# Expert 1 in one piece: block products for a whole expert behind the late half of expert 0, in a fused scan and mixture-of-experts kernel

## The chip, the cores and the metric

The kernel runs on one core of a Trainium2 chip. The metric is device time in microseconds, the median of several runs. Names of engines are those of the profile: PE multiplies matrices (PEld is its weight loading, which overlaps), DVE is the vector engine, ACT the scalar engine, POOL the general engine that also issues the gathers and scatters of rows, SP the queue that issues the plain transfers.

## The reference

Two blocks in a row. The first is a state-space scan over 4 batches, 8 heads and 768 positions, with 32 values and 16 states per head. Its output, 3072 rows of 256 values, is the input of a router: each row goes to the one of 8 experts whose embedding is nearest by cosine, and the row's result is the expert's two-layer network, scaled by the softmax weight of the chosen expert.

```python
xn = x / (np.linalg.norm(x, axis=-1, keepdims=True) + 1e-06)
logits = xn @ en.T / tau
expert_idx = np.argmax(logits, axis=1)
...
for e in range(E):
    mask = expert_idx == e
    h = np.maximum(x[mask] @ w1[e], 0.0)
    out[mask] = gate_w[mask, None] * (h @ w2[e])
```

Each expert has w1 of 256 x 1024 and w2 of 1024 x 256, all in float32. How many rows an expert gets depends on the data.

## The kernel before, in words

**The scan** (`mamba`, line 758) goes through the 768 positions in six chunks of 128. Each chunk ends with rows of 264 values: 256 outputs and 8 logits. `send_rows` writes the rows of a chunk (four batches x 128) to a table in device memory, `y_rows`.

**The routing** runs beside the scan, two or three chunks behind. `pick` finds the expert of each row, `count_picks` adds up the counts (POOL), `rank_rows` and `keep_ranks` give each row its rank within its expert (PE, then ACT), `places` turns ranks into one-hot tiles (DVE), and `locate` multiplies these (PE), which gives for each expert and each of its places the number of the row that belongs there. An expert has 4 tiles of 104 places. `end_places` (line 696) adds the parts of all chunks, transposes them with one product (`table`, line 692), and `to_rows` (line 708) makes two integer tables of that: `gi`, the rows to gather, and `to`, the rows of the output to write.

**Early and late halves.** The first two tiles of experts 0 and 1 can be filled from the first three chunks alone; `early_places` makes a table `gi0` for them while the scan still runs, and `gather_halves` gathers their rows on POOL. So the order of PE after the scan is

1. expert 0, early half: 8 up-projections `up(f)` (each two matmuls over 208 rows), mixed in `scan_end` (line 912) with the end of the routing; then `down(0)` and `down(1)`, 8 matmuls each;
2. expert 1, early half, the same way;
3. expert 0, late half, and expert 1, late half (`moe`, line 1377), for the two tiles each that could be filled only after the last table product;
4. experts 2 to 7, sorted by size, each whole (up to 416 rows).

**Block products.** Experts 2 to 7 use `up_blocks` and `down_blocks` (lines 1182, 1257): the matrices are split into 2 x 2 blocks and multiplied in seven block products in place of eight. A block product of the up-projection is four matmuls, so an expert has 28 + 28 matmuls of about 208 columns in place of 32 + 32. For that DVE makes four sums of blocks of w1 (`sum_w1`), of x (`sum_x`), of w2 (`sum_w2`) and of the hidden values (`sum_h`), and adds products up.

**Gates.** The class `Gates` (line 1326) makes the row weights from the gathered logits: squares (ACT), a power (POOL), differences and scales (DVE), `exp` (ACT), sums and reciprocals (DVE).

**Order.** These parts are written under a manual schedule: each engine runs its instructions in the order of the code, and waits in place. Weights come through SP in the order of the calls of `load_weights`; three buffers each hold w1 and w2. `hold` delays a transfer until a given instruction is done. POOL issues gathers (line 996) and the scatters of results (line 1317) in code order too.

Of the kernel before, what the change touches and what calls it, by code (L numbers as in the profile page):

```python
# [17 lines left out]
Q = 128  # L18
# [592 lines left out]
def keep_ranks(k, c):  # L611
    k.at[c] = k.work.tile([128, NB, E], F32, name="rk", tag="rk")
    k.nc.scalar.copy(out=k.at[c][:].rearrange("p b e -> p (b e)"), in_=k.pz[1][:, 392 : 392 + NB * E])
# [82 lines left out]
def end_places(k):  # L696
    nc = k.nc
    n = k.pz[1][:, 456 : 456 + E]
    nc.tensor.matmul(n, lhsT=k.ones[:], rhs=k.pre[:, NU, :], start=True, stop=True)
    nc.vector.tensor_copy(out=k.idx[:], in_=table(k))  # L700
    k.gi = k.const.tile([TR, E * NT], I32, name="gi")
    k.to = k.const.tile([TR, E * NT], I32, name="to")
    to_rows(k, k.idx[:, 0 : FIXED * NT], 0)
    k.n = k.const.tile([128, E], F32, name="n")
    nc.vector.tensor_copy(out=k.n[:], in_=n)


def to_rows(k, idx, at):
    nc = k.nc
    n = idx.shape[1]  # L710
    r = slice(at, at + n)
    nc.vector.tensor_scalar(out=k.gi[:, r], in0=idx, scalar1=-1.0, scalar2=0.0, op0=ALU.add, op1=ALU.max)
    none = k.mc.tile([TR, n], F32, name=f"none{at}")
    nc.vector.tensor_scalar(
        out=none[:], in0=idx, scalar1=0.0, scalar2=float(T + 1), op0=ALU.is_equal, op1=ALU.mult
    )
    out_rows(k, k.mc, k.gi[:, r], k.to[:, r], none[:], f"to{at}")


def sort_experts(k):  # L720
# [33 lines left out]
    nc.vector.reduce_sum(out=idx[:], in_=rows[:].rearrange("p s t e -> p (s t) e"), axis=AX.X)  # L754
    to_rows(k, idx[:], FIXED * NT)


def mamba(k):
# [41 lines left out]
    for c in range(NC):  # L800
# [50 lines left out]
        if c == NC - 1:  # L851
            k.early_x = early_rows(k)
            gather_halves(k, k.early_x, k.gi0, 0, 0, 3 * NB * Q)
        if c >= 2:
            count_picks(k, c - 2)
        if c == NC - 1:
            gather_halves(k, k.early_x, k.gi0, 0, 1, 3 * NB * Q)
            add_located(k, c - 3)
# [20 lines left out]
        if c == NC - 1:  # L879
            early = early_jobs(k)  # L880
            early[0].turn_x()
            rank_rows(k, c - 2)
            keep_ranks(k, c - 2)
# [3 lines left out]
        if c == NC - 1:  # L887
            load_weights(k, 0, (1,), early[0].turned)
            hold(k, send_rows(k, c - 1), early[0].turned)
            load_weights(k, 1, (0,), early[0].turned)  # L890
            early[0].w2, early[1].w1 = k.w2t[0], k.w1t[1]
# [20 lines left out]
def scan_end(k, early):  # L912

    nc = k.nc
    c = NC - 1
    first, second = early
    gates = Gates(k, k.ep, k.early_x, TR, NT)
    first.up(0)
    rank_rows(k, c - 1)
    keep_ranks(k, c - 1)  # L920
    first.up(1)
    finish(k, c)
    keep_rows(k, c)
    send_rows(k, c)
    load_weights(k, 1, (1,))
    second.w2 = k.w2t[1]
    places(k, c - 1)
    pick(k, c)
    count_picks(k, c)
    first.up(2)  # L930
    gates.square(0)
    first.up(3)
    gates.square(1)
    locate(k, c - 2, True, False)
    locate(k, c - 1, False, False)
    first.up(4)
    rank_rows(k, c)
    keep_ranks(k, c)
    places(k, c)
    for f in (5, 6):  # L940
        first.up(f)
        gates.square(f - 3)
    gates.power()
    gates.largest()
    gates.scale()
    first.up(7)
    second.turn_x()
    gates.exp()
    first.down(0)
    locate(k, c, False, True)  # L950
    end_places(k)
    late = late_jobs(k)
    first.down(1)
    g = gates.end()
    first.gate, second.gate = g[:, 0:HT], g[:, HT:]
    first.to, second.to = k.to[:, 0:HT], k.to[:, NT : NT + HT]
    for f in range(KF):
        second.up(f)
        if 1 <= f <= HT:
            first.out(f - 1)  # L960
        if f == HT:
            sort_experts(k)
            load_weights(k, FIXED)
    second.down(0)
    late[0].turn_x()
    second.down(1)
    k.step = k.ints("step", [128, LEFT], [[1, LEFT]], 0, 0)
    k.part = k.ints("part", [128, 1], [[0, 1]], 0, 1)
    return late
# [16 lines left out]
def early_rows(k):  # L986
    return k.ep.tile([TR, 2 * HT, KD * Y1], F32, name="xg", tag="xg", bufs=2)


def gather_halves(k, x, gi, t, e, rows=T):  # L990
    for i in range(HT):
        gather(k, x[:, HT * e + i, 0:W], gi[:, NT * e + t + i : NT * e + t + i + 1], rows)
# [41 lines left out]
def early_jobs(k):  # L1034
    k.pgs.close()
    ps = k.late_psum.enter_context(k.tc.tile_pool(name="early_ps", bufs=4, space=PSUM))
    k.next_bank = lambda: ps.tile([128, 512], F32, name="eb", tag="eb")
    jobs = []
    for e in range(2):
        j = Job(k, HT, TR, k.w1t.get(e), k.w2t.get(e), k.ep, k.next_bank)  # L1040
        j.x = k.early_x[:, HT * e : HT * e + HT, :]
        jobs.append(j)
    return jobs


def late_jobs(k):
    x = k.late_x = early_rows(k)
    for e in range(2):
        gather_halves(k, x, k.gi, HT, e)
    jobs = []  # L1050
    for e in range(2):
        j = Job(k, HT, TR, k.w1t[e], k.w2t[e], k.ep, k.next_bank)
        j.x = x[:, HT * e : HT * e + HT, :]
        j.to = k.to[:, NT * e + HT : NT * e + NT]
        jobs.append(j)
    return jobs


class Job:
# [41 lines left out]
    def up(s, f):  # L1101
# [8 lines left out]
        if f % 2 == 0 or s.bank_ is not None:  # L1110
# [4 lines left out]
    def down(s, j, half=None, fs=range(KF)):  # L1115
# [14 lines left out]
        if j % 2 == 0:  # L1130
# [246 lines left out]
def moe(k, second, late):  # L1377
# [6 lines left out]
    jobs = list(late)  # L1384
    for j in [second] + jobs:
        j.bank_ = None
    last, e, left = second, 1, leftover_blocks(k)
    for i in range(2):
        j = jobs[i]
        x = k.late_x if i == 0 else jobs[2].x  # L1390
        gates = Gates(k, k.ep if i == 0 else k.p, x, TR, NT)
        for f in range(KF):
            j.up(f)
            if 1 <= f <= last.nt:
                last.out(f - 1)
            if f == 3:
                e += 1
                jobs.append(begin(e))
            if 3 <= f < 7:
                gates.square(f - 3)  # L1400
        gates.power()
        gates.largest()
        last, n = j, jobs[i + 1]
        n.turn_x()
        gates.scale()
        gates.exp()
        j.down(0)
        g = gates.end()
        if i == 0:
            late[0].gate, late[1].gate = g[:, 0:HT], g[:, HT:]  # L1410
        else:
            n.gate = g
        j.down(1)
        if i == 1:
            n.sum_x()
            n.sum_w1(range(4))
        load_weights(k, i + 3)
    gates = None
    for i in range(2, E):
# [208 lines left out]
def kernel(  # L1628
# [24 lines left out]
    with ExitStack() as m:  # L1653
# [9 lines left out]
        with tc.manual_schedule():  # L1663
            early = mamba(k)
            late = scan_end(k, early)
    with (
# [4 lines left out]
        with tc.manual_schedule():  # L1671
            last = moe(k, early[1], late)
# [46 lines left out]
```

## Time and profile before

| what | value |
|---|---|
| time, median of 3 runs | 258.27 us (258.21 to 261.93) |
| the profiled execution | 262.64 us |
| its span, first to last instruction | 260.8 us |
| PE busy | 246.0 us (94%) |
| DVE, ACT, POOL busy | 66%, 46%, 47% |
| mean granted PE clock | 0.969 |
| traffic | 35.93 MB, mean 138 GB/s |

The page gives busy time per engine, the span in 40 slices, the DMA queues, the chain of work that ended last, and the costliest groups of instructions. Further views of the trace give the instructions in order of time and busy times by stage. A PE record for a float32 matmul appears twice, so that one matmul of 208 columns is two records. Times in the views count from the first instruction of the span.

### The profile page before, as it was taken

To read this page: it belongs to the slowest core of one execution; us is meant where nothing else is said; L and a number is where in the kernel's file an instruction comes from. 1 tells how busy PE (TensorE), PEld (TensorE's weight loads), DVE (VectorE), ACT (ScalarE), POOL (GpSimd) and SP (SyncE) were. 2 spreads that over 40 slices of the span, in tenths; PEclk is the share of its full clock that TensorE was granted. 3 is DMA by queue.
4 is the path that set the end of the run, shared out by engine and by line. 5 is a ranking of instruction groups with operands and counts; after the bars stand their busy time and mean duration, and the time that the engine had idled before them with its cause. 6 is when DMAs were issued, how large, how long until landed. Compare 5 with 4: busy or idle time off the path is not lost.

```text
span 260.8 us, 6970 instructions
## 1 busy us (share of the span) xinstructions
PE 246.0 (94%) x2692; PEld 222.6 (85%) x2692; DVE 171.7 (66%) x460; ACT 118.7 (46%) x344; POOL 121.8 (47%) x164
## 2 busy tenths in 40 slices
PE   7897999999699999999999999999999999999991
PEld 2676877878579899999979999999998998999890
DVE  6735689888455460334597896987988889784221
ACT  3524566774137041413255267248428427537400
POOL 5896373473702370648354138418525625125032
PEclk9979799999959999999999999999999999999998
DMA  4945476546299439498932393294176201001001
GB/s 141 326 146 196 147 249 190 182 134 157 70 263 269 139 86 241 153 218 237 220 122 70 77 260 88 49 260 130 52 187 189 74 5 40 24 0 40 23 20 39
DMA packets 22548, 35.93 MB, mean 138 GB/s; under 512 B 2777, under 2 KB 15780, under 8 KB 22512
## 3 DMA queue, kind: packets, MB, share of 16 engines
q1 hardware_dynamic: 19264, 28.73, 39.2%
q0 software_dynamic: 3088, 6.67, 9.6%
q8 instruction: 22, 0.36, 0.6%
q14 instruction: 14, 0.11, 0.1%
q10 hardware_dynamic: 160, 0.06, 0.1%
HBM read 29.05 MB, written 6.50 MB: 136 GB/s over the span
## 4 chain that ended last, share of the span: by engine, by line
PE 44%; issue 24%; POOL 16%; DVE 7%; DMA 5%; another core or an unknown queue 1%; POOLq 1%; ACT 1%; DVEq 0%; SPq 0%; ACTq 0%
POOL xg L996 8%; PE eb L1107 5%; POOL out_dram L1317 5%; PE pg L371 5%; DMA out_dram<-yo,to 4%; PE eb L1125 4%; PE yp L1194 4%; DVE g L381 4%; PE yp L1266 4%; PE hp L1107 3%; PE yp L1125 2%; PE hp L1194 2%; PE pz L438 2%; PE py L422 2%
## 5 line engine op out<-in xcount | busy, mean ns | idle before, releaser
L1317 POOL DMA_INDIRECT out_dram<-yo,to x32 | 34.0, 1061 | 66.1 <-ACT yo L1314 36.2
L996 POOL DMA_INDIRECT xg<-y_rows,gi x32 | 37.3, 1166 | 17.3 <-issue 9.1
L381 DVE TENSOR_TENSOR g<-pg,mask 128x1536 f32<-128x1536 f32 x12 | 21.1, 1757 | 10.0 <-PE pg L371 10.0
L1212 ACT ACTIVATE hT<-hT 128x416 f32<-128x416 f32 (+5 forms) x36 | 19.0, 532 | 12.6 <-DVE hT L1216 6.2
L1125 PE MATMUL yp<-hT,w 128*128 128x208 f32 (+1 forms) x128 | 22.1, 329 | 0.6 <-ACT hT L1212 0.6
L1125 PEld LDWEIGHTS yp<-hT,w 128*128 128x128 f32 x128 | 21.1, 190 | 0.8 <-ACT hT L1212 0.8
L1266 PE MATMUL yp<-T,S 128*128 128x208 f32 (+4 forms) x120 | 21.8, 332 | 0.0
L1266 PEld LDWEIGHTS yp<-T,S 128*128 128x128 f32 x120 | 20.4, 190 | 0.0
L1216 DVE TENSOR_TENSOR hT<-hp,u 128x416 f32<-128x416 f32 (+5 forms) x24 | 13.3, 564 | 10.6 <-PE hp L1194 4.3
L1344 POOL TENSOR_TENSOR gr<-gr,half 104x4 f32<-104x4 f32 x8 | 9.7, 1210 | 21.7 <-ACT sq L1338 21.6
L1194 PE MATMUL yp<-T,S 128*128 128x208 f32 (+5 forms) x96 | 18.6, 336 | 0.4 <-DVE S L1151 0.3
L283 POOL TENSOR_TENSOR xs<-x,rT 128x1024 f32<-128x1024 f32 x6 | 11.9, 1980 | 10.8 <-issue 7.6
L1194 PEld LDWEIGHTS yp<-T,S 128*128 128x128 f32 x96 | 15.4, 190 | 1.7 <-ACT u L1207 1.1
L1107 PE MATMUL eb<-xT,w 128*128 128x208 f32 x64 | 14.5, 375 | 2.2 <-ACT xT L1097 2.2
L1207 ACT COPY p<-yp 128x416 f32<-128x416 f32 (+5 forms) x12 | 5.7, 478 | 21.0 <-PE yp L1194 21.0
L1266 PE MATMUL yp<-hT,w 128*128 128x208 f32 (+4 forms) x80 | 15.1, 331 | 0.0
L1107 PEld LDWEIGHTS eb<-xT,w 128*128 128x128 f32 x64 | 12.0, 207 | 2.5 <-ACT xT L1097 2.3
L1266 PEld LDWEIGHTS yp<-hT,w 128*128 128x128 f32 x80 | 13.7, 190 | 0.0
L1338 ACT ACTIVATE sq<-xg 104x256 f32<-104x256 f32 x32 | 13.0, 408 | 0.0
L1107 PE MATMUL hp<-xT,w 128*128 128x208 f32 x64 | 12.2, 339 | 0.0
L433 ACT COPY yT<-py 128x512 f32<-128x512 f32 x12 | 6.5, 593 | 12.4 <-PE py L422 12.4
L1207 ACT COPY u<-yp 128x416 f32<-128x416 f32 (+5 forms) x24 | 11.5, 484 | 1.3 <-PE yp L1194 0.9
(285 smaller groups left out, 588.8 us busy)
## 6 DMA issues: line engine op xcount, KB each, us to landing
w<-in_moe_w_dram SPq DMA_DIRECT2D x32, 256.0 KB
w<-in_moe_w_dram SPq DMA_DIRECT2D x8, 1024.0 KB
y_rows<-rows SPq DMA_DIRECT2D x6, 528.0 KB
x<-in_x_dram SPq DMA_DIRECT2D x6, 512.0 KB
ct<-in_CT_dram SPq DMA_DIRECT2D x6, 256.0 KB
bi<-in_BT_dram SPq DMA_DIRECT2D x6, 256.0 KB
b<-in_B_dram SPq DMA_DIRECT2D x6, 256.0 KB
xa<-in_x_dram SPq DMA_DIRECT2D x6, 128.0 KB
```

The costliest lines, as they stand in the source:

```text
L371: t.paired = k.nc.tensor.matmul(k.pg[:, q, 192 * u + a : 192 * u + a + n], lhsT=m, rhs=x, start=True, stop=True, tile_position=(32 * q, 0),)
L381: t.masked = k.nc.vector.tensor_tensor(out=g[:], in0=k.pg[:, :, 0:384].rearrange("p q (u m) -> p q u m", u=2), in1=k.mask[:].unsqueeze(1). ...
L996: k.nc.gpsimd.indirect_dma_start(out=x, out_offset=None, in_=k.y_d[0:rows, :], in_offset=bass.IndirectOffsetOnAxis(ap=at, axis=0), bounds_ ...
L1107: nc.tensor.matmul(t, lhsT=s.w1[:, j, 128 * f : 128 * f + 128], rhs=s.xT[:, j, 0:m], start=(j == 0), stop=(j == KD - 1))
L1125: nc.tensor.matmul(t, lhsT=s.w2[:, f, 128 * j : 128 * j + 128], rhs=s.hT[:, f, r], start=(f == 0), stop=(f == KF - 1))
L1194: nc.tensor.matmul(t[:, m * u : m * u + m], lhsT=w[:, f : f + 128], rhs=x, start=start and u == 0, stop=True, skip_group_check=True,)
L1207: nc.scalar.copy(out=p[:, 0 : 2 * m], in_=t[:, 0 : 2 * m])
L1212: nc.scalar.activation(h, h, ACT.Relu)
L1216: nc.vector.tensor_tensor(out=h, in0=view(t), in1=view(p), op=ALU.add)
L1266: nc.tensor.matmul(t, lhsT=a[:, f], rhs=b[:, f], start=start and f == 0, stop=(f == 3), skip_group_check=True)
L1317: d = nc.gpsimd.indirect_dma_start(out=k.out[:, :], out_offset=bass.IndirectOffsetOnAxis(ap=s.to[:p, i : i + 1], axis=0), in_=y[:p], in_of ...
L1338: s.k.nc.scalar.activation(sq[:], s.x[:, i, :].rearrange("p (j w) -> p j w", j=KD)[:, :, 0:128], ACT.Square, accum_out=s.r[:, i : i + 1],)
```

## The change

- Expert 0 keeps its early and late halves (`early_job`, `late_job`). Expert 1 no longer has halves: `whole_job` makes one job of 4 tiles. Two of these are gathered with the early table `gi0`, now after the first gates' power in `scan_end` and no longer during the last chunk of the scan; the other two after the last table.
- Expert 1 uses `up_blocks` and `down_blocks`, like experts 2 to 7, and comes after expert 0's late half.
- `to_rows` is split: `from_rows` makes `gi` first, the gathers are issued, and `to_rows` makes `to` after that.
- The last `locate` and `end_places` stand inside expert 0's `down(0)`, after two and after four of its eight matmuls. After the early half, PE goes straight on to expert 0's late half.
- The early gates' largest, scale and exp stand after `end_places`, and cover two tiles; the sorting of the experts follows.
- Expert 1's w1 is loaded after the last ranks are kept (`k.ranked`), behind the last rows on SP; its w2 after the late half's transposed x is copied.
- Relus and copies of jobs in the early pool go to ACT throughout.

```diff
 def end_places(k, whole):
...
+    idx = k.idx[:, 0 : FIXED * NT]
+    from_rows(k, idx, 0)
+    late = late_job(k)
+    gather_tiles(k, whole.x[:, HT:], k.gi, NT + HT)
+    to_rows(k, idx, 0)
...
@@ scan_end
     gates.square(1)
+    gates.power()
+    whole = whole_job(k)
+    gather_tiles(k, whole.x[:, 0:HT], k.gi0, NT, 3 * NB * Q)
     locate(k, c - 2, True, False)
...
     keep_ranks(k, c)
+    load_weights(k, 1, (0,), k.ranked)
     places(k, c)
-    for f in (5, 6):
+    for f in (5, 6, 7):
         first.up(f)
-        gates.square(f - 3)
-    gates.power()
+    first.down(0, fs=range(2))
+    locate(k, c, False, True)
+    first.down(0, fs=range(2, 4))
+    late = end_places(k, whole)
+    first.down(0, fs=range(4, KF))
     gates.largest()
     gates.scale()
-    first.up(7)
-    second.turn_x()
     gates.exp()
-    first.down(0)
-    locate(k, c, False, True)
-    end_places(k)
-    late = late_jobs(k)
+    first.gate = gates.end()
+    first.to = k.to[:, 0:HT]
+    sort_experts(k)
     first.down(1)
...
+    late.turn_x()
+    load_weights(k, 1, (1,), late.turned)
+    late.w2, whole.w1, whole.w2 = k.w2t[0], k.w1t[1], k.w2t[1]
+    load_weights(k, FIXED)
...
@@ moe
+    gates = Gates(k, k.ep, k.late_x, TR, HT)
+    for f in range(KF):
+        late.up(f)
+        if 1 <= f <= HT:
+            last.out(f - 1)
+        if f == 3:
+            e += 1
+            jobs.append(begin(e))
+        if f in (4, 6):
+            gates.square(f // 2 - 2)
+    gates.power()
+    gates.largest()
+    whole.sum_w1(range(2))
+    late.down(0)
+    whole.turn_x()
+    gates.scale()
+    gates.exp()
+    whole.sum_x()
+    late.gate = gates.end()
+    late.down(1)
+    whole.sum_w1(range(2, 4))
+    load_weights(k, 3)
+    last = late
+    gates = Gates(k, k.p, whole.x, TR, NT)
+    for f in range(NT):
+        gates.square(f)
+    gates.power()
+    gates.largest()
+    gates.scale()
-    for i in range(2, E):
+    for i in range(1, E):
...
+def whole_job(k):
+    j = Job(k, NT, TR, None, None, cols=CAP)
+    j.x = k.ep.tile([TR, NT, KD * Y1], F32, name="x1")
+    return j
```

## The prediction

> **What bounds the kernel now.** I read the page's busy shares first, then a table of busy time by stage, then the chain of work that ended last, then the instructions in order of time where the diff cuts. The page and the stage table:
>
> ```profile
> PE 246.0 (94%) x2692; PEld 222.6 (85%) x2692; DVE 171.7 (66%) x460; ACT 118.7 (46%) x344; POOL 121.8 (47%) x164
> ...
> 83.27:127.31 44.04, 43.77 (x269) 42.47 (x268) 16.83 (x70) 12.27 (x44) 23.16 (x25) 1.00 0.73 188
> 127.31:138.70 11.39, 11.12 (x61) 9.99 (x61) 9.66 (x21) 6.71 (x16) 4.92 (x5) 1.00 0.45 137
> 138.70:149.29 10.59, 10.59 (x66) 10.56 (x66) 9.02 (x17) 4.27 (x14) 2.95 (x3) 1.00 0.26 65
> 149.29:160.00 10.71, 10.71 (x66) 10.28 (x66) 8.84 (x29) 7.20 (x17) 5.23 (x5) 1.00 0.79 205
> ```
>
> The columns of a stage row are length, then busy PE, PEld, DVE, ACT and POOL, then granted clock, DMA share and GB/s. From 83.27 (end of expert 0's early up-projection) to 127.31 (first block product of expert 2) PE is busy 43.77 of 44.04 us, and nothing else exceeds half. So this stretch is worth what PE must do in it, plus any hole that is opened. The three rows below it are block products: expert 2's up, expert 2's down, expert 3's up.
>
> The chain shows the only large hole nearby:
>
> ```profile
> 66.57 3.91 another core or an unknown queue
> 70.48 0.50 ACT xT L1097
> 70.98 0.04 issue
> 71.02 1.76 PE eb L1107 x4
> ```
>
> PE is out of work from 68.8 to 71.02, and the next four matmul records need 1.76 us instead of the 0.70 of later ones: the granted clock falls to 0.5 from 70.5 to 77.3. And the cut itself, in order of time:
>
> ```profile
> 83.27 0.52 PE L1094 MATMUL eb<-ident,xg 104*128 104x104 f32 x4
> 83.63 3.00 PE L1125 MATMUL eb<-hT,w 128*128 128x208 f32 x16
> 83.77 0.29 DVE L659 TENSOR_TENSOR eq<-eq,tok 128x128 f32<-128x128 f32 x1
> 83.83 0.51 ACT L1097 COPY xT<-eb 128x416 f32<-128x416 f32 x1
> 86.56 0.39 PE L669 MATMUL pz<-hot,eq 128*32 128x104 f32 x8
> 87.01 0.26 DVE L690 TENSOR_TENSOR idx_t<-idx_t,pz 128x104 f32<-128x104 f32 x1 [1.71 <-PE pz L669]
> 87.33 0.37 PE L692 MATMUL pz<-same,idx_t 128*104 128x32 f32 x2 [0.27 <-DVE idx_t L690]
> 87.53 3.06 PE L1125 MATMUL eb<-hT,w 128*128 128x208 f32 x16
> 87.74 0.19 DVE L700 COPY idx<-pz 104x32 f32<-104x32 f32 x1 [0.46 <-PE pz L692]
> 87.96 0.17 DVE L712 TENSOR_SCALAR gi<-idx 104x8 int32<-104x8 f32 x1
> 88.45 1.15 POOL L996 DMA_INDIRECT xg<-y_rows,gi  x1 [3.79 <-DVE to_c L1007]
> 89.90 1.08 POOL L996 DMA_INDIRECT xg<-y_rows,gi  x1 [0.30 <-issue]
> 90.43 1.57 PE L1107 MATMUL eb<-xT,w 128*128 128x208 f32 x8
> ```
>
> The late rows can be gathered only after the last table product (L692). Their transposes stand at 99.31; expert 1's early half (90.43 to 99.31) covers the gathers. A 208-column matmul is two records; eight start in 83.63 to 86.56 and occupy 2.83 us (the chain's figure for x16), 0.353 each.
>
> [...] 6.83 us at 0.5, two windows, after one in which PE was busy 1.78 of 3.42. [...] Here the second early gather's issue ended at 66.02, its packets were over at 67.6, and the transposes began at 68.24: 1.6 to 2.2 us.
>
> **The change, part by part**, in the profiled run's time.
>
> (1) **Expert 1 in block products.** Before, experts 0 and 1 take four halves of 32 matmuls of 208 columns: 128. After, expert 0 keeps two halves (64) and expert 1 takes 28 + 28: 120. Eight fewer at 0.353: **-2.83 us**, all on PE in a PE-bound stretch. Input and output transposes are as many as before; two output tiles move later, a shift and not a cost.
>
> (2) **Holes that close.** The 44.04 us hold 112 matmuls (39.5), transposes of inputs (1.8) and of six output tiles (1.3), locate, count and table (0.4): 43.0 of work. 0.27 of the rest is the wait at L692; the other handoffs I leave as they are. After, two matmuls (0.71) stand between the locate product and the table, against 0.45 + 0.28 of DVE latency (86.56 to 87.01 to 87.33): **-0.27**. Expert 2's up is 11.39 us for 28 x 0.353 + 0.44 = 10.32 of work; the 1.07 excess is the first block expert's, whose sums on DVE (S at L1151, T at L1163) started late, behind a wait for POOL's power (L1344). Expert 3's excess is only 0.17. After, expert 1 is the first; two of its sums are made earlier, but its gates put scale and exp just ahead of its first products on DVE and ACT. Between 0.17 and 1.07 I take 0.5, plus 0.17 for expert 2: **-0.40**.
>
> (3) **The late gather loses its cover.** After, PE runs two matmuls of down(0), locate, two more, the table, then 4 + 8 matmuls, then the late transposes. From 83.27: +0.71 = 83.98; eq is ready at 84.06, locate starts at 84.1 and ends at 84.3; two matmuls to 85.0; count and table to 85.25. By the intervals above, idx is copied 0.41 after the table's start (85.46), gi at 85.68 to 85.85, the gather 0.32 later at 86.17. The second starts 1.45 later (87.62) and its issue ends at 88.70. Landed after 1.6 to 2.2: 90.3 to 90.9; I take 90.5. PE ends its 12 matmuls (4.24) at 89.49. Then transposes to ACT copy 0.56, copy 0.51, handoff 0.04: the late half's first matmul at 91.6, where without holes it would be 89.49 + 0.36 = 89.85. **+1.75** (1.55 to 2.15).
> Who stands ahead on POOL: count_picks (80.06 to 81.09), a power (1.05, to 82.15), and the two new gathers of expert 1's early rows (each 1.08 + 0.30, to 85.0), clear of 86.17 by about a microsecond. If those slip, each us is a us.
>
> (4) **The clock.** PE then has 2.0 us without dense matmuls (89.49 to 91.6, transposes 0.36 in it). A window of 0.52 busy (67.08 to 70.50) lost the clock, one of 0.82 (15.88 to 19.30) kept it[...]. Cost: nothing, or a window at half rate, 3.41 / 2 = 1.7. Unknown; I take the middle, **+0.85**. Nothing excludes either end.
>
> (5) **Moves hidden.** Two early gathers leave POOL at 67.66 to 70.13: taken at 0, since the transposes then need only the first two; from -1.65 (see rivals). On SP, expert 1's w1 (4 issues, 2.6 us) goes behind the rows of the last chunk and the last ranks (81.4): landed by about 86, used first by sums near 98. Its w2 waits for the late transposes (about 91.5); queued behind it on SP are expert 2's weights, used near 118. Both 0; without the cover, the delay itself. Relus and copies that move from DVE to ACT (0.34 each, in a pitch of 0.71) and one more small set of gate steps (POOL 1.05): 0 beside PE.
>
> **Sum:** -2.83 - 0.27 - 0.40 + 1.75 + 0.85 = **-0.90 us**. The profiled execution took 262.64 (span 260.80 and 1.84 around it): 261.7 after. It stands 4.37 above the median of 258.27, mostly its half-clock stretch before 77.3 (some 3.3), ahead of every step costed; so **257.4** against the median.
>
> **Rivals.**
> A. *As above*, 257.4; by the clock's ends 256.5 to 258.3. Chance 0.45.
> B. *The early stage gains too.* ACT's xT waits until 70.48, though its inputs landed by 67.6; the third gather's packets end near 70.1. If that is the cause, dropping it starts expert 0 up to 1.65 earlier: 255.8. Against: the releaser is unknown, and no instruction there waits for the third gather. Or the clock holds at (4). 0.22.
> C. [...] At late.turn_x, should landing take 2.6 us of hole and the hole straddle a window, two windows at half clock cost 3.41: -3.50 + 2.6 + 3.4 = +2.5, **260.8**. It decides once hole plus clock exceed the 3.50 of gains. For: the same thing at 68.8 to 77.3. Against: full dense work follows at once. 0.20.
> D. *DVE and ACT become the bound of expert 1's up*, where exp waits for scale, scale for power, and p1's copy stands behind it: +1.6 instead of -0.40: 259.4. For: DVE busy 9.66 of 11.39 in that stage already. 0.13.
>
> **Numbers.** Leaving out the outer tails of B and C, the range is 255.3 to 260.4. A measurement tells about 2% (5.2 us) from no change; A to D lie inside it. Faster by more than 2% needs B and more, 0.03; slower by more needs C repeated, 0.05.
>
> **What would show it.** Right: a PE hole of 1 to 2 us released by xT ahead of the late half; 120 matmuls where there were 128; expert 2's up at about 10.5. Clock row: a 5 near 92 or none. Wrong: the hole above 3 us, or POOL still on expert 1's gathers at 86; weights ending a wait; expert 1's up above 12 us.

## The result and the profile after

The changed kernel takes **256.97 us** in the median (255.27 to 261.29, 20 runs), the kernel before 258.37 us in the 20 runs beside it. The ratio is **0.9925 [0.9899, 0.9951]**, about 1.9 us less; in a second comparison, 256.09 us, it was 0.9913 [0.9883, 0.9943]. Both lie inside 2%. The forecast was 257.4. The ratios are of undisturbed runs alone and the medians of all, which is why the two medians do not give the ratio.

The page of after, busy times and the row of the granted clock in 40 slices:

```profile
PE 237.7 (93%) x2676; PEld 215.3 (85%) x2676; DVE 182.9 (72%) x481; ACT 125.0 (49%) x356; POOL 124.7 (49%) x165
...
PEclk9999999999999999999999999999999999999998
```

PE has 2676 records where it had 2692: 16 fewer, which are the eight matmuls. The span is 254.2 us and the execution 255.98. No slice shows half a clock. The profiled execution of before has four windows of 3.41 us at half clock ahead of its end (two in the scan, from 12.5 and 26.1, and two up to 77.3), so the difference of the two profiled spans, 6.6 us, is not the worth of the change. A second profile of before, the first experiment, has none of these and a span of 256.4.

Busy time by stage of after (columns as before: length, then PE, PEld, DVE, ACT, POOL, then clock, DMA share, GB/s): the late hole; expert 0's late half; expert 1's up; expert 1's down; expert 2's up.

```profile
83.30:85.41 2.11, 1.03 (x7) 0.43 (x5) 1.90 (x10) 0.84 (x2) 1.78 (x3) 1.00 0.29 84
85.41:98.03 12.62, 12.62 (x77) 12.35 (x78) 5.22 (x17) 4.17 (x15) 7.94 (x11) 1.00 0.97 277
98.03:110.91 12.88, 10.86 (x61) 9.96 (x61) 9.36 (x26) 7.99 (x23) 7.82 (x7) 1.00 0.93 228
110.91:121.50 10.59, 10.59 (x66) 10.56 (x66) 9.02 (x17) 4.28 (x14) 2.06 (x2) 1.00 0.21 55
121.50:132.30 10.80, 10.80 (x65) 10.35 (x65) 8.81 (x29) 7.28 (x17) 5.28 (x5) 1.00 0.76 194
```

PE is busy throughout three of the five rows. It idles in the first, which was foreseen, and in the third: expert 1's up takes 12.88 us with PE busy for 10.86, where expert 2's takes 10.80.

PE of after, in order of time, at the three places that the prediction costed: the start of expert 0, the late hole, and expert 1's up.

```profile
67.39 0.97 PE L1106 MATMUL eb<-xT,w 128*128 128x208 f32 x4 [0.55 <-ACT xT L1096]
...
83.66 0.31 PE L1093 MATMUL eb<-ident,xg 104*128 104x104 f32 x1
84.33 0.49 PE L1093 MATMUL eb<-ident,xg 104*128 104x104 f32 x3 [0.35 <-DMA xg<-y_rows,gi]
85.41 1.67 PE L1106 MATMUL hp<-xT,w 128*128 128x208 f32 x8 [0.59 <-ACT xT L1096]
...
103.45 0.43 PE L1310 MATMUL ot<-ident,yoT 128*104 128x128 f32 x2 [2.02 <-ACT yo L1313]
```

At the start of expert 0 the 2.2-us wait for xT that before had is gone; 0.55 is the time of one copy. The late hole, from the end of the matmuls at 83.30 to 85.41, ends on the gathered rows and then on the copy of xT. The wait of 2.02 us at 103.45 is the one the prediction did not have. PE stands at an output transpose (L1310), which needs a bank of the accumulator that ACT's scaling of the previous output tile (L1313) has still to read. The chain of the work that ended last, in that stretch of after, says what held ACT:

```profile
99.56 2.17 POOL gr L1343
...
102.40 0.03 ACT gl L1365
...
102.54 0.49 ACT p L1206
103.02 0.39 ACT yo L1313
...
103.45 0.43 PE ot L1310 x2
```

The columns are start, length and what ran; each piece releases the next. The power of expert 1's gates on POOL ends at 101.73, the scale on DVE follows, then `exp` on ACT at 102.40. Behind `exp` in ACT's order stand the copy of p (L1206) and the scaling of the output tile, and behind that PE.

From the second profile of before (span 256.4) to after (254.2) the 2.2 us go as follows. The times are those of the first gather of early rows, of expert 0's first up and first down matmul, of expert 3's first block product, and of the end.

| stretch | before, second profile | after | difference |
|---|---|---|---|
| start to the first early gather | 61.70 | 60.66 | -1.04 |
| to expert 0's up | 7.75 | 6.73 | -1.02 |
| to expert 0's first down | 9.81 | 9.44 | -0.37 |
| to expert 3's up | 65.67 | 66.14 | +0.47 |
| to the end | 111.52 | 111.26 | -0.26 |

The first row lies ahead of anything the diff touches and varies from profile to profile (60.6 to 62.2, and 63.0 and 63.3 in the two with two half-rate windows in the scan). Without it this pair of profiles shows 1.2 us. The third row is the transposes of expert 1's early rows, which moved to the fourth. That fourth row, with the whole of expert 1 in it, **gained nothing**.

### The profile page after: what moved, and what is told of

Read it like the earlier page. It is cut to its first block, busy times and chain, and to the rows that moved or that the text cites. A ratio compares the mean times of both kernels' runs of the same rounds, so it can differ in the third digit from the quotient of the medians.

```text
span 254.2 us, 6984 instructions
## 1 busy us (share of the span) xinstructions
PE 237.7 (93%) x2676; PEld 215.3 (85%) x2676; DVE 182.9 (72%) x481; ACT 125.0 (49%) x356; POOL 124.7 (49%) x165
## 4 chain that ended last, share of the span: by engine, by line
PE 48%; issue 16%; POOL 13%; DVE 9%; DMA 6%; ACT 5%; POOLq 1%; ACTq 1%; DVEq 0%
PE yp L1265 19%; PE yp L1193 10%; PE hp L1193 7%; DMA out_dram<-yo,to 5%; POOL xg L997 3%; DVE g L381 3%; PE eb L1106 3%; POOL out_dram L1316 2%; POOL xb L298 2%; DMA xg<-y_rows,gi 2%; PE yp L1093 2%; PE pg L371 1%; ACT u L1206 1%; POOL gr L1343 1%; DVE V L355 1%
## 5 line engine op out<-in xcount | busy, mean ns | idle before, releaser
L997 POOL DMA_INDIRECT xg<-y_rows,gi x28 | 33.4, 1195 | 13.8 <-issue 7.3
L1211 ACT ACTIVATE hT<-hT 128x416 f32<-128x416 f32 (+5 forms) x42 | 22.4, 535 | 10.2 <-DVE hT L1215 9.2
L1265 PE MATMUL yp<-T,S 128*128 128x208 f32 (+4 forms) x144 | 26.4, 333 | 0.0
L1265 PEld LDWEIGHTS yp<-T,S 128*128 128x128 f32 x144 | 24.6, 190 | 0.0
L1343 POOL TENSOR_TENSOR gr<-gr,half 104x4 f32<-104x4 f32 (+1 forms) x9 | 10.9, 1213 | 24.6 <-ACT sq L1337 24.6
L1206 ACT COPY p<-yp 128x416 f32<-128x416 f32 (+5 forms) x14 | 6.7, 478 | 24.9 <-PE yp L1193 24.9
L1193 PEld LDWEIGHTS yp<-T,S 128*128 128x128 f32 x112 | 18.3, 190 | 0.6 <-ACT u L1206 0.6
L1265 PE MATMUL yp<-hT,w 128*128 128x208 f32 (+4 forms) x96 | 18.2, 333 | 0.0
L1124 PE MATMUL yp<-hT,w 128*128 128x208 f32 (+1 forms) x96 | 16.4, 326 | 0.5 <-ACT hT L1211 0.5
L1206 ACT COPY u<-yp 128x416 f32<-128x416 f32 (+5 forms) x28 | 13.6, 489 | 3.0 <-PE yp L1193 2.8
L1162 DVE TENSOR_TENSOR T<-hT 128x832 f32<-128x832 f32 (+4 forms) x12 | 11.9, 990 | 3.6 <-ACT hT L1211 3.6
L1162 DVE TENSOR_TENSOR T<-hT,T 128x832 f32<-128x832 f32 (+4 forms) x12 | 11.9, 989 | 0.2
L1193 PE MATMUL yp<-T,w 128*128 128x208 f32 (+5 forms) x56 | 11.2, 344 | 0.3 <-ACT u L1206 0.2
```

Source lines behind the costliest of these rows:

```text
L997: k.nc.gpsimd.indirect_dma_start(out=x, out_offset=None, in_=k.y_d[0:rows, :], in_offset=bass.IndirectOffsetOnAxis(ap=at, axis=0), bounds_ ...
L1124: nc.tensor.matmul(t, lhsT=s.w2[:, f, 128 * j : 128 * j + 128], rhs=s.hT[:, f, r], start=(f == 0), stop=(f == KF - 1))
L1162: s.k.nc.vector.tensor_tensor(out=T[n], in0=x, in1=y, op=ALU.subtract)
L1193: nc.tensor.matmul(t[:, m * u : m * u + m], lhsT=w[:, f : f + 128], rhs=x, start=start and u == 0, stop=True, skip_group_check=True,)
L1206: nc.scalar.copy(out=p[:, 0 : 2 * m], in_=t[:, 0 : 2 * m])
L1211: nc.scalar.activation(h, h, ACT.Relu)
```

## The experiments

Of all these kernels none leaves out work of the reference; one adds matmuls that nobody reads. Ratios are to the kernel before on the same chip.

**1. The kernel before, once more.** No edit. It asks whether its wait for xT belongs to the kernel or to the half clock of the first profile.

> The kernel before, unchanged, profiled once more: where does its time lie when PE keeps its clock from 66 to 78? Theory (the 4.37 us between the profiled execution and the median are the half-clock windows from 70.5 to 77.3 and the 1.65 us that ACT waited too long for xT): in an undisturbed execution xT follows the early transposes within about 0.1 us and the span is near 256.5. Rival (the wait for xT belongs to the kernel: it lasts until the third early gather has landed): xT again starts 1.5 us or more after the transposes, whatever the clock does.

Measured: 258.29 us, span 256.4, no half clock there. PE in order of time, and the copy on ACT:

```profile
66.62 0.58 PE L1094 MATMUL eb<-ident,xg 104*128 104x104 f32 x4
...
69.45 0.79 PE L1107 MATMUL eb<-xT,w 128*128 128x208 f32 x3 [2.22 <-ACT xT L1097]
```

```profile
68.90 0.51 ACT L1097 COPY xT<-eb 128x416 f32<-128x416 f32 x1 [6.21 <-remote]
```

The transposes are recorded at 66.62, yet ACT starts to copy their result at 68.90, and the releaser is given only as "remote". The wait belongs to the kernel, and the theory that a run without the half clock would not have it fell.

**2. The same kernel with `exp` later.** In `moe`, expert 1 alone gets its `exp` after the fourth step of its up-projection in place of the first. A step is half a block product, two matmuls; the recorded text calls the steps block products.

```diff
-            if f == 0 and gates is not None:
+            if f == (3 if i == 1 else 0) and gates is not None:
                 gates.exp()
-            elif f == 3:
+            if f == 3:
```

> The changed kernel, with the exp of expert 1's gates moved on ACT from after its first block product to after its fourth (just ahead of the sum that needs it). Theory (the 2.02 us hole of PE ahead of the second output transpose at 103.45 comes from that exp: it waits for DVE's scale, which waits for POOL's power, and ACT's copy of p1 and the output tile yo that frees the bank ot stand behind it): the hole goes, expert 1's up-projection falls from 12.88 to about 10.6 us, the median from 256.97 to about 255.0, ratio to before about 0.987. Rival (the power on POOL and the scale on DVE hold the stage, exp only shows it; the wait moves to DVE's first hidden sum): the stage stays above 12 us and the median within 0.5 us of 256.97.

Measured: 254.40 us, ratio **0.9822 [0.9789, 0.9855]**. PE at the same place, and the stage of expert 1's up:

```profile
100.72 0.38 PE L1310 MATMUL ot<-ident,yoT 128*104 128x128 f32 x2
```

```profile
97.29:108.75 11.46, 11.20 (x61) 9.86 (x61) 9.33 (x27) 7.61 (x24) 7.33 (x6) 1.00 1.03 254
```

The output transpose no longer waits, and expert 1's up is 11.46 where it was 12.88. So `exp`, standing on ACT for the power, made the hole. This kernel beats both others, and is 1.0% under after. The stage fell less than was expected (about 10.6), the ratio more: 1.0% is 2.7 us, the stage 1.42. Each ratio is uncertain by 0.7 to 0.9 us. A half-rate window, which a hole of this size cost in two of five profiles (last section), may be a part of the rest; that is not shown, since neither profile compared here has one.

**3. After, with the output tile in another bank.** `exp` stays where the change has it; the second output tile is transposed into a bank of `yp` rather than the one the first still occupies.

```diff
-        t = s.bank("ot", 1) if s.p is not None or i % 2 == 0 else s.bank("yp", 4)
+        t = s.bank("ot", 1) if i % 2 == 0 else s.bank("yp", 4)
```

> The changed kernel, with exp where the change has it, and with the second output tile of expert 0's late half transposed into one of the four banks yp, not into the single bank ot. Theory (PE waits at 103.45 for the bank ot, which ACT frees late): the 2.02 us hole at the second output transpose goes. But exp still holds ACT, and PE then waits where the second block of p1 must be copied out: the up-projection of expert 1 falls only to about 11.5 to 12, the median by about 1 us, ratio about 0.988. Rival A (nothing else waits for ACT soon enough): the stage falls to 10.6 and the ratio to 0.984. Rival B (the hole only moves): ratio 0.9925 as the changed kernel.

Measured: 254.91 us, 0.9864 [0.9798, 0.9929], from four runs. PE at that place:

```profile
103.15 0.97 PE L1193 MATMUL yp<-T,S 128*128 128x208 f32 x4 [0.71 <-ACT p L1206]
```

The hole shrinks to 0.71 and moves to the block product that needs the copy of p, the next thing behind `exp` on ACT. So two things made the 2.02: ACT's order, and one bank that tied PE's transposes to it. With both edits at once:

> The changed kernel with both edits to expert 1's up-projection: exp after its fourth block product, and the second output tile in a bank of yp. Theory (exp's place alone held ACT; once it is moved the bank is no longer waited for): as with exp alone, ratio 0.982 within 0.003. Rival (the bank still costs a part of the 1.1 us by which that stage exceeds its 10.3 us of PE work: its second transpose waits 0.2 to 0.5 us): 0.5 us better, ratio 0.980.

Measured: 254.11 us, 0.9826 [0.9794, 0.9859], expert 1's up 11.66. Beside 0.9822 that is nothing more: once `exp` stands out of the way, the bank does not matter.

**4. Expert 1's late gathers ahead of expert 0's.** In `end_places` the order of the two calls is exchanged, which puts two issues of POOL ahead of the rows that PE waits for.

```diff
-    late = late_job(k)
     gather_tiles(k, whole.x[:, HT:], k.gi, NT + HT)
+    late = late_job(k)
```

> The changed kernel with the two gathers of expert 1's late rows issued ahead of those of expert 0's late half, so that the latter start 2.77 us later (two times 1.08 + 0.30). Theory (the gather stands on the path at the late transposes): the hole grows from 2.11 to about 4.9 us, the median to about 259.7 (+2.8). Rival A (a hole this long also costs the clock: one or two windows, 1.7 to 3.4 more): 261.4 to 263. Rival B (the gathered rows are not what the late half waits for): no change, 257.0.

Measured: 261.42 us, 1.0081 [1.0046, 1.0116], some 4.0 us above after (0.0156 of 258.4). PE in order of time:

```profile
85.09 0.31 PE L1093 MATMUL eb<-ident,xg 104*128 104x104 f32 x1 [2.19 <-DMA xg<-y_rows,gi]
86.63 0.49 PE L1093 MATMUL eb<-ident,xg 104*128 104x104 f32 x3 [1.24 <-DMA xg<-y_rows,gi]
```

Counted from expert 0's first down matmul the late half starts after 11.52 us, against 8.47 to 8.61 in after and its relatives: 2.9 to 3.1 later. Then the clock falls to half from 87.92 to 91.33, and once more in expert 1's up, from 108.4 to 111.8. So the price of rival C is real, hole and window both, but only for a hole some 2.8 us longer (two issues of 1.08 with 0.30 after each) than the change makes.

**5. Four unread matmuls in the late hole.** Three ahead of the late transposes and one behind, by weights and x that are there already.

```diff
     first.down(1)
+    spare = k.next_bank()
+    fill_pe(k, first, spare, 3)
     late.turn_x()
+    fill_pe(k, first, spare, 1)
```

> The changed kernel with four matmuls of 208 columns that nobody reads put into the PE hole ahead of expert 0's late half: three before the late transposes, one after them (1.41 us of dense work in a hole of 2.11). Output and all other work unchanged. Theory (the hole costs PE its clock for a window in about half of the executions, 0.85 us in the median): the hole is not idle any more, the median falls by 0.5 to 0.9 to about 256.3, and the mean granted clock rises. Rival (dense work on both sides keeps the clock at full rate, the hole costs only its own length): 256.97 within 0.4, or later by what the added matmuls overrun.

Measured: 255.86 us, 0.9894 [0.985, 0.9938], which overlaps after's 0.9925. The late half starts at 85.01 (after: 85.41 and 85.05). Since none of the nine profiles with the late gathers placed as in after (this one among them) lost the clock at that hole, there was nothing for the filling to save. It tells only that it costs nothing measurable.

**6. Expert 1's early gathers back to their old place.** After, but `whole_job` and its two early gathers stand in `mamba` behind `count_picks(k, c - 2)`, where before has them.

```diff
             count_picks(k, c - 2)
         if c == NC - 1:
+            k.whole = whole_job(k)
+            gather_tiles(k, k.whole.x[:, 0:HT], k.gi0, NT, 3 * NB * Q)
             add_located(k, c - 3)
...
-    whole = whole_job(k)
-    gather_tiles(k, whole.x[:, 0:HT], k.gi0, NT, 3 * NB * Q)
+    whole = k.whole
```

> The changed kernel, with the gathers of expert 1's two early tiles put back on POOL to where the kernel before had gathers: behind the first ranks' counts, while expert 0's early rows are transposed. Theory: the delay comes back, xT 2.2 us after the transposes in place of 0.55; the median rises by 1.0 to 1.65 to about 258.3, ratio to before about 0.998. The gathers ahead of the late ones (75.58 to 78.1 in the changed kernel) vanish, which gains nothing, since POOL stood idle 1.86 us before the late gather. Rival (the early stage is the same either way): ratio 0.9925 as the changed kernel.

Measured: 259.07 us, **1.0001 [0.9965, 1.0037]**. The whole gain of the change is gone. PE and POOL in order of time:

```profile
66.67 0.97 PE L1107 MATMUL eb<-xT,w 128*128 128x208 f32 x4 [0.55 <-ACT xT L1097]
...
69.19 0.19 PE L605 MATMUL pz<-pre,ones_b 128*128 128x32 bf16 x1 [1.53 <-POOL pre L590]
```

```profile
66.40 1.08 POOL L998 DMA_INDIRECT x<-y_rows,gi  x1 [0.30 <-issue]
...
67.88 1.58 POOL L590 TENSOR_TENSOR pre<-pre,ob 128x8 bf16<-128x8 bf16 x4
```

The size was about what was expected, the mechanism not. xT is in time (copied at 66.11) although the third gather is on its way, to land at 67.96. What waits is a rank product of PE (L605): its counts (`count_picks`, L590) stand on POOL behind the two gathers (65.02 and 66.40) and one sum of 0.41 us. One thing differs from before: these gathers write a tile of their own (`x`), where before's write the other half of the tile `xg` that PE is transposing. In this profile the clock also falls to half after that, from 68.91 to 72.3, and again from 106.46 to 109.9, at the hole of expert 1's up.

**7. The kernel before, with those gathers moved, two ways.** First, they are held on POOL until xT is copied:

```diff
-            gather_halves(k, k.early_x, k.gi0, 0, 1, 3 * NB * Q)
             add_located(k, c - 3)
...
             early[0].turn_x()
+            gather_halves(k, k.early_x, k.gi0, 0, 1, 3 * NB * Q, early[0].turned)
```

> The kernel before, with one edit: expert 1's two early gathers on POOL are held until ACT has copied expert 0's transposed early rows (xT), so that no third gather is in flight while these rows are transposed. Theory (the early transposes of the kernel before count as done only when the third gather lands: xT at 68.90 and 70.47 in its two profiles, with the third gather's last landings at 68.94 and 70.61): xT follows the transposes within 0.6 us in place of 2.2 to 2.3, and the median falls by about 1.65 to 0.9936 of the kernel before. Rival (the delay is another one, and the changed kernel is free of it by chance or by its order): xT still 2.2 us after the transposes, ratio 1.00.

Measured: 261.05 us, 1.0128 [1.0073, 1.0183]. xT came 0.5 us after the transposes, but the counts stood behind the held gathers: PE waited 2.57 us for them at 71.24, and the clock fell for a window. The edit's own new wait hides what it was to measure, so it settles no size. Then, no hold, only POOL's order: the two gathers go behind both counts.

```diff
             count_picks(k, c - 2)
         if c == NC - 1:
-            gather_halves(k, k.early_x, k.gi0, 0, 1, 3 * NB * Q)
             add_located(k, c - 3)
...
             count_picks(k, c - 1)
+            gather_halves(k, k.early_x, k.gi0, 0, 1, 3 * NB * Q)
```

> The kernel before, with one edit in the order of POOL: expert 1's two early gathers are issued behind both counts (count_picks of the last two chunks) instead of ahead of the second. No wait is added; the gathered rows are needed some 9 us later. Theory (in the early stage the kernel before pays for these two gathers ahead of the count: PE's rank product needs the count, and xT comes 2.2 us after its transposes; the changed kernel is free of both): PE starts expert 0's up-projection and its ranks 1.0 to 1.65 us earlier, ratio 0.994 to 0.996. Rival (the early stage is bound otherwise, and the changed kernel's gain comes all from expert 1): ratio 1.00 within 0.002.

Measured: 256.58 us, **0.9910 [0.9877, 0.9943]**. PE:

```profile
67.16 0.58 PE L1094 MATMUL eb<-ident,xg 104*128 104x104 f32 x4
...
68.33 0.44 PE L1107 MATMUL eb<-xT,w 128*128 128x208 f32 x1 [0.55 <-ACT xT L1097]
```

```profile
66.66 1.03 POOL L590 TENSOR_TENSOR pre<-pre,ob 128x8 bf16<-128x8 bf16 x4 [0.28 <-DVE ob L585]
```

xT is in time, and no product waits for the counts, which POOL does at 66.66, ahead of the two gathers (68.27 and 69.65). One call, moved behind the second count, gives what the whole change gives (after beside it: 0.9913). From the first gather to expert 0's up it takes 6.10 us in place of 7.75. By the ratio 2.3 was gained; its interval, 1.5 to 3.2, holds that 1.65.

**8. The changed kernel again,** beside the last:

> The changed kernel, unchanged, beside the other two on the same chip, for comparison with them: about 0.9925 of the kernel before. In its profile the hole at the late transposes is 1.4 to 1.8 us beyond the transposes, and PE waits 2.0 us for the bank ot in expert 1's up-projection; both belong to the order of the work, so both are there again. Rival (the 2.0 us were a single execution's): expert 1's up-projection below 11.7 us.

Measured: 256.09 us, 0.9913 [0.9883, 0.9943]. The late half starts at 85.05, the wait of 2.02 us in expert 1's up is there again, and expert 1's up takes 13.13 us.

**9. Expert 1 whole, but in plain products.** With the edit of experiment 2, expert 1 uses `up(f)` and `down` as expert 0's halves do, without any of the sums: 32 matmuls of 416 columns in place of 56 of 208, which is the work of 64 of 208.

```diff
-        for f, _ in enumerate(j.up_blocks()):
+        for f, _ in enumerate(j.up_blocks() if i > 1 else plain_up(j)):
...
-        j.sum_h()
+        if i > 1:
+            j.sum_h()
```

> The changed kernel with the later exp, and with expert 1 whole but in plain products: 16 + 16 matmuls of 416 columns in place of 28 + 28 of 208, and no sums of blocks for it on DVE. Theory (a block product expert saves 8 matmuls of 208 columns on PE, 0.353 each, and nothing else decides): slower than the kernel with the later exp (254.4 of a before of 259.69, ratio 0.982) by 2.8 us, ratio about 0.993. Rival (the sums on DVE cost expert 1 as much as the eight matmuls save): within 1 us of the kernel with the later exp, ratio 0.982 to 0.986.

Measured: 258.05 us, 1.0001 [0.9962, 1.004]. From the late half's end to expert 3's start the profile has 46.71 us, against 43.52 with blocks: 3.19, of which eight matmuls of 208 columns are 2.83. By the ratios the difference is larger, 1.8% or 4.6 us; what the other 1.4 us are I can't say. The slow start of the first expert in blocks moves to expert 2, where PE waits for the same copy:

```profile
125.61 0.62 PE L1193 MATMUL yp<-T,S 128*128 128x208 f32 x2 [0.75 <-ACT p L1206]
```

**10. Expert 1's last two sums of w1 earlier.** In after they run on DVE at 99.57 and 100.17, beside the power of expert 1's gates. Here all four are made at 91 to 93.5, where DVE is idle.

```diff
-    whole.sum_w1(range(2))
+    whole.sum_w1(range(4))
     late.down(0)
...
-    whole.sum_w1(range(2, 4))
```

> The changed kernel, but expert 1's last two sums of w1 (two DVE instructions of 0.68 us with two inputs in SBUF each, at 99.57 and 100.17 in after) are made together with the first two at 89 to 92, where DVE then has 4.5 us idle. In after they run beside the power of expert 1's gates on POOL (99.56), which takes 2.16 us where others take 1.05; in the kernel with expert 1 in plain products, without sums there, the power took 1.01. Theory: the sums hold POOL up. Then the power takes about 1.05, scale, exp and the copy of p come 1.1 us earlier, the PE wait of 2.02 at the output transpose falls to about 0.9, expert 1's up to about 11.8, and the ratio to before falls from 0.9925 to about 0.988. Rival: the power is slow for another reason (the first after a row of gathers), and the sums are only beside it: it stays at 2.16, the wait at 2.0, the ratio at 0.9925. Earlier sums cost nothing on PE, since the weights are there by 89 already; if they are not, DVE's copies of xT at 95.03 and with them expert 1's start come later.

Measured: 255.79 us, **0.988 [0.9829, 0.993]**. POOL's power, and PE at the output transpose:

```profile
101.75 1.01 POOL L1343 TENSOR_TENSOR gr<-gr,half 104x4 f32<-104x4 f32 x1 [2.93 <-ACT sq L1337]
```

```profile
104.49 0.43 PE L1310 MATMUL ot<-ident,yoT 128*104 128x128 f32 x2 [0.86 <-ACT yo L1313]
```

The power takes 1.01 in place of 2.16, and PE's wait falls from 2.02 to 0.86, by as much. Expert 1's up goes from 12.88 to 12.13 (99.81 to 111.94): a little less was won than the 1.1 expected, since PE here waits 0.40 at the output transpose before. The interval reaches after's 0.9925; it is the trace that decides.

## Why the prediction was right in its time and wrong in two of its steps

The time of 257.4 was met within 0.5 us. The change itself was forecast at -0.9 and measured at -1.9. That they lie so near is partly luck: term (2) was too low by 1.9, (4) too high by 0.85 and (5) too high by some 2. The 4.37 us between the profiled run and the median were laid mostly on the half clock before 77.3; that profile has two more half-rate windows in the scan, but as a difference of two measured times the 4.37 stand.

| step | predicted | measured |
|---|---|---|
| (1) eight matmuls fewer | -2.83 | -2.83 by count of records; experiment 9's profile has 3.19 for the blocks as a whole |
| (2) holes that close | -0.27 - 0.40 | -0.27: the table product stands at 78.88 without a wait; but the first block expert's excess is 2.57 against 1.07: **+1.5** |
| (3) late gather | +1.75 | 2.11 of hole less 0.36 of transposes: **+1.75** |
| (4) clock | +0.85 | 0: no half-rate window at the late hole, in both profiles of after and seven of its relatives |
| (5) moves hidden | 0, from -1.65 | the early order on POOL is worth **-2.0 to -2.3** by ratio, -1.0 to -1.65 in the traces |

**(1)** held, to the count.

**(3)** held in all its parts. The prediction's clock starts at 83.27 where after's first down matmul stands at 76.83, 6.44 earlier. Shifted by that, the first late gather was issued at 86.41 (predicted 86.17), the second was out at 88.88 (88.70), PE ran out at 89.74 (89.49), and the late half began at 91.85 (91.6). POOL, in order of time:

```profile
77.03 1.08 POOL L997 DMA_INDIRECT x<-y_rows,gi  x1 [0.30 <-issue]
79.97 1.08 POOL L997 DMA_INDIRECT xg<-y_rows,gi  x1 [1.86 <-DVE to_c L1008]
81.36 1.08 POOL L997 DMA_INDIRECT xg<-y_rows,gi  x1 [0.30 <-issue]
```

POOL was free of expert 1's early gathers 1.86 us before it was wanted, where about one was expected. From the end of the second issue (82.44) to the transpose of its rows (84.33) it takes 1.9 us, in the middle of the 1.6 to 2.2 that before's own gathers showed.

**(2) failed, and it is the term that ate the gain.** Expert 1's up has 28 x 0.353 + 0.43 for output transposes = 10.31 of work in 12.88 us, so an excess of 2.57; 2.02 of it are the hole. The prediction's words were "its gates put scale and exp just ahead of its first products on DVE and ACT", and then 0.5 was taken between the two excesses that the profile showed, 0.17 and 1.07. But the bracket was made of experts that don't have these gates there, so it was no bracket for one that does. The prediction's own sign of being wrong, "expert 1's up above 12 us", came true. Rival D had the right place, order and size: `exp` waits for scale, scale for the power, p's copy stands behind `exp`, +1.6. Its one omission is the output transpose that shares a bank, which is where PE in fact stood (experiment 3). What made the power late can be followed back further in order of time. POOL issues four gathers of expert 2's rows until 96.27; only then comes the power of expert 0's late gates (96.29), whose scale lets ACT do that expert's `exp` at 97.67, after a wait of 2.66. Expert 1's four squares stand behind that on ACT (97.79 to 99.49), and then its power at 99.56, 1.5 us after PE began expert 1 (98.03). It took 2.16 us, where the median of the nine is 1.05, since two sums of DVE ran beside it (experiment 10). Experiment 2 returns 1.42 of the 2.57 in the profile.

**(5) failed in the other direction.** Of the two gathers that leave POOL the prediction said "taken at 0, since the transposes then need only the first two". It asked who needs the rows, and not, for this move, who stands *behind* the issue on POOL, which was asked with care at the late gathers. The counts do, and PE's rank product behind them. Taking the move back costs the whole gain (experiment 6), and making it alone yields the whole gain (experiment 7). The second rank product tells it best: it starts 8.59 us after the first early gather in before (second profile) and 8.53 in experiment 6, and 6.93 in experiment 7. In before PE stood at xT ahead of it, in experiment 6 at the counts; but before's counts ended at 8.35 too, so they alone would have held the product nearly as long. Each of the two ratios is uncertain by some 0.9 us, and so the 2.0 to 2.3 are not clearly larger than the 1.0 to 1.65 that the traces show ahead of expert 0; half-clock windows behind such waits, as in experiment 6's profile, may add to it, which was not separated. The weights' moves that were taken at 0 were 0: the sums of expert 1's w1 start at 89.11 without a wait, and PE is busy for all of the 12.62 us in which the moved weights arrive. The "one more small set of gate steps" was not: it is the power at 96.29 and the `exp` at 97.67 that stand ahead of expert 1's squares under (2).

**What stays open.** Rival B was right that the early stage gains. Its mechanism, a third gather that holds up expert 0's rows, is neither shown nor excluded. In both profiles of before ACT copies xT 1.7 us after the recorded end of the transposes. The semaphore events in the traces say that ACT waited for PE: the count that PE raises after these transposes comes at 68.87 and 70.44, 1.68 and 1.63 after their recorded end and 0.02 ahead of the copy. In the twelve other profiles it comes 0.01 to 0.02 after that end. What held PE is not shown. The first pieces of the third gather land at 68.18 and 69.72, about 0.7 ahead of the late counts. Experiment 6 has a third gather at the same place in time and no delay of xT, but its gather writes another tile, so it does not exclude the rival; in experiment 7 the gather comes later.

**(4)** The clock was a fair unknown with a value in the middle. For a hole of after's size, 2.11 us, nothing is what it cost; in experiment 4, with the late half 2.9 to 3.1 us later, the clock was at half from 87.92 to 91.33. That PE's busy share of a window decides was the author's assumption, and the bracket set on it, 0.52 busy lost and 0.82 kept, does not hold: in the same profile of before a window of 0.91 (9.06 to 12.47) lost the clock too.

Together: -2.83 - 0.27 + 1.5 + 1.75 = +0.15 for the whole of what the change is about, near the +0.1 of the table's third and fourth rows together; and the early order, an incidental part, gives -2.0 to -2.3. Measured: -1.9.

## What to carry to other kernels

When a transfer is moved on a queue, ask two questions of each place, old and new: who needs its data, and which instructions stand behind its issue and who waits for those; here two issues that moved behind the counts held all of the gain. A saving of matmuls is paid out only if the side work that comes with the new form (gates, sums, copies) is not put ahead of the copies that PE needs at once: bound such a start by building the chain of its own instructions, and not by the excess of stages that lack them. And separate the parts of a change that seems neutral: this one held about 0 and about -2 us, and moving one `exp` gave some 2.7 more (ratio 0.9822 against 0.9925).

## What the runs showed of the hardware

- **The busy share of a window did not tell whether the clock was lost.** Every half-rate stretch ahead of the kernels' ends lasts 3.41 us, or 6.83 in the first profile of before. In that profile the three of them start at 12.47, 26.12 and 70.50, which is 4 and 13 times 3.41 apart; a window here is a stretch of 3.41 on such a grid. In after the half rate at its end starts at 251.72, and counted back from there the window at the 2.02 hole is 101.53 to 104.94, with PE busy for 1.49 of it. The windows just ahead of a lost clock were not idle: PE was busy for 0.25 (held gathers), 0.29 and 0.41 (experiment 4), 0.41 and 0.47 (experiment 6), and 0.52 (before) of them. In the scan, among small products, even windows of 0.76 and 0.91 (before) and 0.78 (both edits of experiment 3) lost it. Windows of 0.44 (after, at the 2.02 hole), 0.53 (experiment 4) and 0.55 (before again) kept it. The same hole of 2.02 us in expert 1's up lost the clock in two of five profiles (experiments 4 and 6): the window that held it was 0.41 busy there, and 0.44 to 0.66 in the three that kept the clock (after, after again, experiment 5).
- **Two sums on DVE held up a power on POOL.** The power of 104 x 4 values takes 2.16 us with two sums of 0.68 beside it (2.17 with `exp` late, where they stand there too), and 1.01 without them, in experiment 10, where they are elsewhere, and in experiment 9, where there are none. The sums keep their 0.68; it is the power that is held up. So a 1.36-us pair of sums, counted as hidden beside PE, cost 1.15 us on the chain.
- **The issues of gathers, not their landings, ordered POOL.** An issue of 104 rows mostly held POOL for 1.08 us, with 0.30 to the next, whoever waited. In experiment 6 the sum behind the fourth gather's issue (66.40 to 67.48) starts at 67.52, while the third gather lands only at 67.96. The late rows are there 1.9 us after the issue's end, in after (82.44 to 84.33) as in experiment 4 (83.21 to 85.09); the early rows of after took 2.9 (63.37 to 66.31).
